# Windowed attention followed by an ELU feed-forward layer on one core: the first steps re-ordered around pair 3, one more subtraction on ScalarE, and the last products and rows cut another way

## The chip, the cores and the metric

The kernel runs on one core of a Trainium2 chip. The metric is the device time of one execution in microseconds. The core has TensorE (matrix products and the weight loads ahead of them), VectorE (called DVE in the profile), ScalarE (ACT), GpSimd (POOL) and SyncE (SP). Each engine takes its own instructions strictly in the order written; semaphores hold an instruction until what it reads is there. SP, ACT and POOL also issue DMA transfers, which all run on the core's 16 DMA engines.

## The reference

Attention for 8 batches and 8 heads of 576 positions by 64, where a position sees only those within 32 of it; then a feed-forward layer over the 4608 rows of 512, with an ELU between its two products.

```
scores = scale * q @ k.T ; masked where |i - j| > 32 ; attn = softmax(scores)
x   = (attn @ v), rows of all heads side by side     # 4608 x 512
h   = x @ w_in                                        # 512 -> 2048
g   = where(h > 0, h, exp(min(h, 0)) - 1)             # ELU
out = g @ w_out                                       # 2048 -> 512
```

The kernel computes the ELU as min(max(h, 0), exp(h) - 1), which is the same, and the products in bfloat16.

## The kernel before

**Attention in pairs.** The queries are cut into blocks of 64, 72 in all; two blocks make a pair (36 pairs), and a pair gives 128 rows of x. A pair goes through these functions: `scores` (16 narrow products, in two banks of PSUM), `exponential` on ACT, `mask` on DVE (a product with 0 and 1), `pv` (16 narrow products with the values, whose extra column of ones gives the sums), `normalize` on DVE (a reciprocal, then a product), `x_transpose` on TensorE (four transposes into PSUM) and `x_evac`, ACT's copy of them into the tile xT. Later pairs transpose by DMA. `rotate_v` makes on DVE the copy of the values shifted by 64 rows, V_o, in two parts, that the odd blocks read.

**The feed-forward layer in steps.** The rows go in 18 groups (t) of 256, two pairs each; 2048 hidden columns are cut into 8 steps of 256. That makes 144 steps. `order` says which group and slice step kk is: the first four slices of group 0, the first four of group 1, the other four of both in turn, then group by group. Step kk issues `mm1(kk)`: 8 products of 128 x 256 into the PSUM tile h0 or h1 (alternating), the exponential e_sb on ACT (L609), and the subtraction of 1, m_sb, on DVE (L615), for step 1 on ACT (L613). One step later `elu(kk)` forms g_sb on DVE (L626), which reads PSUM and frees it for `mm1(kk + 2)`. Two steps later `mm2(kk)` adds 4 products of 128 x 512 to the two PSUM tiles psY (L640). With the last slice of a group, `mm2` copies both blocks of 128 rows to SBUF, on ACT and DVE, and sends them out.

**Order around the change.** It is written out by hand. `at(kk, slot, fn, ...)` puts work into a step, and the main loop at the end runs for each kk: slot "first"; `elu(kk - 1)`; slot "dve"; `mm1(kk)`; slot "mid"; the products `mm2` that are due; slot "end". `mm2` runs two steps behind, with a table of exceptions for the first steps, since w_out's first quarter arrives late: none at 2 and 4, steps 0 and 1 at 3, steps 2 and 3 at 5. Pairs 0 and 1 are done before the loop; pairs 2 and 3 share steps 0 to 3 and make the rows of group 1, which step 4 reads first. `idle` is a number of products on zeros that only keep TensorE at work. They fill places where it waits.

The lines of pairs 2 and 3 before the change are L485 to L499. As written, DVE does at step 0 rotate part 0, mask of pair 2, rotate part 1, mask of pair 3, and only then, at step 1, the ELU of step 0; TensorE does mm1(0), the scores, mm1(1), four idle products, pv(2), two idle, pv(3), one idle, mm1(2), mm1(3), both pairs' transposes, then mm2(0) and mm2(1).

**Weights.** They come in quarters on POOL's queue, cast on the way: w_in's second quarter serves slices 2 and 3, which steps 2, 3, 6 and 7 read; w_out's first quarter serves slices 0 and 1, the `mm2` of steps 0, 1, 4 and 5. POOL issues them among loads of values; it waits for earlier transfers before it can issue more.

**The end.** The last step (143) has its PSUM in two tiles, of 128 hidden columns for 256 rows each, with two exponentials, subtractions and ELUs of half width. In the main loop the products of steps 142 and 143 are issued together: for the first row block (`ts` 0) those of both steps, then for the second. After each block its rows are copied out: the first by DVE, the second in two column halves, the left by DVE and the right by ACT, sent by SP and ACT.

Of the kernel before, what the change touches and what calls it, by code (L numbers as in the profile page):

```python
# [9 lines left out]
FP32 = mybir.dt.float32  # L10
# [11 lines left out]
def kernel(  # L22
# [9 lines left out]
    nc = tc.nc  # L32
# [5 lines left out]
    D_MODEL = H * D  # L38
# [8 lines left out]
    VS = 5  # L47
# [184 lines left out]
    def copy_on(eng, d_, s_):  # L232
        if eng is nc.scalar:
            nc.scalar.copy(d_, s_)  # L234
        else:
            eng.tensor_copy(d_, s_)  # L236
# [232 lines left out]
    def at(kk, slot, fn, *args):  # L469
        tasks.setdefault((kk, slot), []).append((fn, args))  # L470
# [15 lines left out]
    at(0, "mid", scores, 3, "u")  # L486
    for i in (2, 3):
        at(0, "mid", exponential, i)
    for i in (2, 3):
        at(0, "mid", rotate_v, 0, 2, VS - 1, (i - 2,))  # L490
        at(0, "mid", mask, i)

        at(1, "mid", idle, (4, 2)[i - 2], "y1")
        at(1, "mid", pv, i)
        at(2, "dve", normalize, i)
        at(3, "mid", x_transpose, i)
        at(3, "mid", x_evac, i, nc.scalar)
    at(1, "end", idle, 1, "y1")
    at(4, "dve", swap_pools)  # L499

    for part, kq in ((HALF_A, 7), (HALF_B, 15)):
# [86 lines left out]
    def mm1(kk):  # L588
        t, s = order[kk]
        h = kk % 2  # L590


        tags = (f"h{h}", "s") if kk == NSTEP - 1 else (f"h{h}",)
        w = FG // len(tags)
        psH[kk], m_t[kk] = [], []
        for z, tag in enumerate(tags):
            ps = ps_tile([128, w, TT], FP32, tag, "ps")
            psH[kk].append(ps)
            for j in range(w):
                fo = s * FG + z * w + j  # L600
                for do in range(NDO):
                    nc.tensor.matmul(  # L602
                        ps[:, j, :],
                        lhsT=w_in_sb[:, do, fo * 128:(fo + 1) * 128],
                        rhs=xT[t][:, :, do, :],
                        start=(do == 0), stop=(do == NDO - 1))
        for z, ps in enumerate(psH[kk]):
            e_sb = mpool.tile([128, w, TT], FP32, tag="e_sb", name="e_sb")
            nc.scalar.activation(e_sb, ps, AX.Exp)  # L609
            m_sb = mpool.tile([128, w, TT], BF16, tag="m_sb", name="m_sb")  # L610
            if kk == 1:

                nc.scalar.activation(m_sb, e_sb, AX.Copy, bias=-1.0)  # L613
            else:
                nc.vector.tensor_scalar(m_sb, e_sb, -1.0, None, ALU.add)  # L615
            m_t[kk].append(m_sb)
            if kk == NSTEP - 1:
                elu(kk, z)
# [10 lines left out]

    out_t = out.rearrange("(t ts p) c -> t p ts c", p=128, ts=TT // 128)  # L630

    def mm2(kk, parts=(0, 1)):
        t, s = order[kk]
        if s == 0:
            psY[t] = [ps_tile([128, D_MODEL], FP32, g, "psY")
                      for g in (("h2", "t0") if t == 1 else ("y0", "y1"))]
        last = t == NT - 1 and s == STEPS - 1
        for ts in parts:
            for j in range(FG):
                nc.tensor.matmul(  # L640
                    psY[t][ts],
                    lhsT=g_t[kk][:, j, ts * 128:(ts + 1) * 128],
                    rhs=w_out_sb[:, s * FG + j, :],
                    start=(s == 0 and j == 0),
                    stop=(s == STEPS - 1 and j == FG - 1))
        if last and s == STEPS - 1:


            for ts in parts:
                for z in range(1 + ts):  # L650
                    c = slice(z * D_MODEL // 2 * ts,
                              D_MODEL if z == ts else D_MODEL // 2)
                    eng = (nc.vector, nc.scalar)[z]
                    y_sb = opool.tile([128, D_MODEL], FP32,
                                      tag=f"y_sb{1 - z}", name="y_sb")
                    copy_on(eng, y_sb[:, c], psY[t][ts][:, c])
                    (nc.scalar if z else nc.sync).dma_start(
                        out_t[t, :, ts, c], y_sb[:, c])
        elif s == STEPS - 1:
            for ts in range(2):  # L660
                eng = (nc.scalar, nc.vector)[ts]
                y_sb = opool.tile([128, D_MODEL], FP32, tag=f"y_sb{ts}",
                                  name="y_sb")
                copy_on(eng, y_sb, psY[t][ts])
                nc.sync.dma_start(out_t[t, :, ts, :], y_sb)

    LAG = 2
    for kk in range(NSTEP + LAG):
        run(kk, "first")
        if 1 <= kk < NSTEP:  # L670
            elu(kk - 1)
        run(kk, "dve")
        if kk < NSTEP:
            mm1(kk)
        run(kk, "mid")

        for n in {2: (), 3: (0, 1), 4: (), 5: (2, 3)}.get(
                kk, (kk - LAG,) if kk >= LAG else ()):

            if n < NSTEP - 2:  # L680
                mm2(n)
            elif n == NSTEP - 1:
                for ts in range(2):
                    for m in (n - 1, n):
                        mm2(m, (ts,))
        run(kk, "end")


# [28 lines left out]
```

The softmax here doesn't subtract the row's maximum and nothing guards it: scores larger than these inputs give would overflow.

## Time and profile before

| what | value |
| --- | --- |
| median of 4 runs | 305.62 us (305.29 to 306.34) |
| profiled execution, its own time | 305.63 us |
| its span | 303.9 us |
| TensorE products, busy | 295.6 us, 97% |
| TensorE weight loads, busy | 197.2 us, 65% |
| VectorE busy | 242.4 us, 80% |
| ScalarE busy | 168.7 us, 56% |
| GpSimd busy | 48.2 us, 16% |
| granted TensorE clock | 1.00 |
| moved by DMA | 52.81 MB |

Times in the profile are microseconds from the start of the span. A row of the timeline gives the start, the length, the engine, the line of the kernel, the operation, the tile written and the tile read; "x8" means that eight like instructions are merged, and brackets give how long the engine stood idle before and what ended that. TensorE's products overlap, so a row's length holds the drain of the last one; how fast they follow each other is read from the starts. PEld is the weight load ahead of a product. The chain is followed back from the last instruction, at each step to what released it.

### The profile page before, as it was taken

How to read it: one execution, taken by the hardware profiler on the slowest of the kernel's cores; microseconds unless marked ns; L12 is line 12 of the kernel's file. 1: busy time of each engine (PE TensorE's matmuls, PEld its weight loads, DVE VectorE, ACT ScalarE, POOL GpSimd, SP SyncE). 2: the span in 40 equal slices, each digit the busy share in tenths (PEclk: the TensorE clock that was granted, in tenths of full speed). 3: DMA queues.
4: the chain of work that ended last, by engine and by line, in shares of the span. 5: the costliest groups of instructions: out<-in, count | busy, mean ns of one | idle time of the engine just before them, and what ended most of it. 6: DMA issues, size and time to landing. Idle time of an engine off the chain costs nothing.

```text
span 303.9 us, 7644 instructions
## 1 busy us (share of the span) xinstructions
PE 295.6 (97%) x3091; PEld 197.2 (65%) x3091; DVE 242.4 (80%) x473; ACT 168.7 (56%) x254; POOL 48.2 (16%) x68
## 2 busy tenths in 40 slices
PE   7799999999999999999999999999999999999995
PEld 2466666677666666666666666666666676666662
DVE  6876687978788887988798879887988787877664
ACT  3654656778664567546754675367545353534331
POOL 8836101820004100230023001300000000000000
PEclk9999999999999999999999999999999999999999
DMA  9999999999765997999799969996931111121011
GB/s 187 184 203 205 191 240 368 344 150 220 178 194 149 296 121 216 242 307 148 154 266 278 216 169 263 324 155 121 274 59 71 35 71 35 72 37 69 2 69 70
DMA packets 92117, 52.81 MB, mean 174 GB/s; under 512 B 76594, under 2 KB 81970, under 8 KB 92082
## 3 DMA queue, kind: packets, MB, share of 16 engines
q1 hardware_dynamic: 47330, 35.61, 43.6%
q0 software_dynamic: 42880, 10.10, 42.4%
q10 hardware_dynamic: 1872, 6.62, 5.8%
q8 instruction: 24, 0.39, 0.6%
q14 instruction: 11, 0.09, 0.1%
HBM read 36.70 MB, written 15.34 MB: 171 GB/s over the span
## 4 chain that ended last, share of the span: by engine, by line
PE 88%; DMA 4%; POOL 3%; DVE 2%; ACT 1%; issue 0%; DVEq 0%; POOLq 0%
PE psY L640 40%; PE ps L602 40%; DMA w_out_sb<-in_moe_w_out_dram 4%; PE psS L336 3%; PE psS L304 3%; POOL Ve L142 1%; PE ptx L279 1%; DVE g_sb L626 1%; POOL c L136 1%; PE psXT L357 1%; POOL w_in_sb L175 0%; DVE m_sb L615 0%; PE ptx L274 0%; ACT e_sb L609 0%; ACT pu L315 0%
## 5 line engine op out<-in xcount | busy, mean ns | idle before, releaser
L609 ACT ACTIVATE e_sb<-ps 128x512 f32<-128x512 f32 (+1 forms) x145 | 86.3, 595 | 119.6 <-PE ps L602 112.0
L602 PE MATMUL ps<-xT,w_in_sb 128*128 128x256 bf16 x1152 | 149.2, 273 | 0.1
L640 PE MATMUL psY<-w_out_sb,g_sb 128*128 128x512 bf16 x576 | 147.5, 379 | 0.2 <-DVE g_sb L626 0.2
L602 PEld LDWEIGHTS <-w_in_sb 128*128 128x128 bf16 x1152 | 110.7, 98 | 38.4 <-DMA w_in_sb<-in_moe_w_in_dram 0.8
L626 DVE SCALAR_TENSOR_TENSOR g_sb<-ps,m_sb 128x512 bf16<-128x512 f32 (+1 forms) x145 | 99.4, 686 | 12.6
L615 DVE TENSOR_SCALAR m_sb<-e_sb 128x512 bf16<-128x512 f32 x144 | 61.9, 430 | 37.9 <-ACT e_sb L609 36.1
L640 PEld LDWEIGHTS <-g_sb 128*128 128x128 bf16 x576 | 54.6, 98 | 39.2 <-DVE g_sb L626 0.6
L142 POOL DMA_DIRECT2D Ve<-in_v_dram x40 | 35.4, 896 | 138.6 <-PE psS L336 79.9
L315 ACT ACTIVATE pu<-psS 128x1024 bf16<-128x1024 f32 x36 | 36.5, 1020 | 1.6 <-PE psS L304 1.6
L348 DVE TENSOR_TENSOR x_st<-psS,rc 128x512 bf16<-128x512 f32 x36 | 24.9, 691 | 1.2
L324 DVE TENSOR_TENSOR pm<-pu,masks 128x1024 bf16<-128x1024 bf16 x36 | 24.6, 683 | 0.6 <-ACT pu L315 0.5
L234 ACT CAST qkb<-f 128x768 bf16<-128x768 f32 (+1 forms) x29 | 25.0, 860 | 0.0
L336 PEld LDWEIGHTS <-pm 128*64 128x64 bf16 x576 | 11.2, 110 | 10.0 <-DVE pm L324 8.8
L336 PE MATMUL psS<-Ve,pm 128*64 128x65 bf16 x320 | 13.6, 196 | 0.9 <-ACT pu L315 0.8
L236 DVE COPY y_sb<-psY 128x512 f32<-128x512 f32 (+1 forms) x19 | 12.7, 670 | 1.0 <-PE psY L640 1.0
L304 PEld LDWEIGHTS <-kT 64*128 64x128 bf16 x576 | 9.6, 95 | 4.9 <-issue 4.0
L336 PE MATMUL psS<-Vo,pm 128*64 128x65 bf16 x256 | 12.0, 196 | 0.2 <-DVE Vo L153 0.2
L304 PE MATMUL psS<-qT,kT 64*128 64x64 bf16 x576 | 11.8, 191 | 0.5 <-DVE kT L236 0.5
L234 ACT COPY y_sb<-psY 128x512 f32<-128x512 f32 (+1 forms) x18 | 10.3, 571 | 3.0 <-DVE y_sb L236 3.0
L153 DVE COPY Vo<-Ve 64x1040 bf16<-64x1040 bf16 x24 | 11.2, 467 | 0.8
L395 PE MATMUL ps_idle<-zeros 128*128 128x512 bf16 x27 | 9.0, 460 | 1.3 <-DVE zeros L194 1.3
L234 ACT COPY qT<-ptx 128x1152 bf16<-128x1152 bf16 (+2 forms) x8 | 7.5, 969 | 3.7 <-PE ptx L279 2.9
(36 smaller groups left out, 71.4 us busy)
## 6 DMA issues: line engine op xcount, KB each, us to landing
out_dram<-y_sb SPq DMA_DIRECT2D x35, 256.0 KB, 3.3
f<-in_q_dram SPq DMA_DIRECT2D x12, 576.0 KB, 5.8
f<-in_k_dram SPq DMA_DIRECT2D x12, 576.0 KB, 8.1
in_dram<-qkb ACTq DMA_DIRECT2D x10, 576.0 KB, 4.2
Ve<-in_v_dram POOLq DMA_DIRECT2D x24, 128.0 KB, 11.3
w_in_sb<-in_moe_w_in_dram POOLq DMA_DIRECT2D x4, 512.0 KB, 10.6
w_out_sb<-in_moe_w_out_dram POOLq DMA_DIRECT2D x4, 512.0 KB, 12.7
Ve<-in_v_dram POOLq DMA_DIRECT2D x16, 96.0 KB, 10.6
```

The source lines that it names most:

```text
L142: nc.gpsimd.dma_start(out=V_e[b % 3][p0:p1, m, :, 0:D], in_=v[b, :, lo + p0:lo + p1, :].rearrange("h p d -> p h d"))
L234: nc.scalar.copy(d_, s_)
L304: nc.tensor.matmul(psS[:, h % 2, hp * 128 + z * QB:hp * 128 + (z + 1) * QB], lhsT=kT[b % 2][base:base + 64, KPAD + hp * S + QB * qb - WIN: ...
L315: nc.scalar.activation(pu, _bap(psS, [psS.ap[0], [1, 1024]]), AX.Exp, scale=SCALE)
L324: nc.vector.tensor_mul(pm, pu, _bap(mm, [mm.ap[0], [0, H], [1, 2 * QB]]))
L336: nc.tensor.matmul(psS[QB * z:QB * (z + 1), par, hp * VD:(hp + 1) * VD], lhsT=pm[:, par * HP + hp, z * QB:(z + 1) * QB], rhs=vv[:, qb // 2 ...
L348: nc.vector.tensor_mul(x_st, _bap(psS, [psS.ap[0], [VD, HP], [512, 2], [1, D]]), _bap(rc, [rc.ap[0], [2, HP], [1, 2], [0, D]]))
L602: nc.tensor.matmul(ps[:, j, :], lhsT=w_in_sb[:, do, fo * 128:(fo + 1) * 128], rhs=xT[t][:, :, do, :], start=(do == 0), stop=(do == NDO - 1))
L609: nc.scalar.activation(e_sb, ps, AX.Exp)
L615: nc.vector.tensor_scalar(m_sb, e_sb, -1.0, None, ALU.add)
L626: nc.vector.scalar_tensor_tensor(g_t[kk][:, z * w:(z + 1) * w, :], ps, 0.0, m_t[kk][z], ALU.max, ALU.min)
L640: nc.tensor.matmul(psY[t][ts], lhsT=g_t[kk][:, j, ts * 128:(ts + 1) * 128], rhs=w_out_sb[:, s * FG + j, :], start=(s == 0 and j == 0), sto ...
```

## The change

For pairs 2 and 3: on DVE the ELU of step 0 comes ahead of pair 3's mask. On TensorE, pv(3) goes behind mm1(2), the idle product after it is gone, and pair 3's transposes go behind mm2(0). Pair 3's normalization follows pv(3) in step 2. The subtraction of step 2 moves to ACT, so that two steps have it there. At the end, mm2 of step 142 is issued whole and then that of step 143. The first row block's copy stays whole on DVE; of the second, ACT now takes the left half and DVE the right.

```diff
--- before.py
+++ after.py
@@ -486,16 +486,21 @@
     at(0, "mid", scores, 3, "u")
     for i in (2, 3):
         at(0, "mid", exponential, i)
+    at(0, "mid", rotate_v, 0, 2, VS - 1, (0,))
+    at(0, "mid", mask, 2)
+    at(0, "mid", rotate_v, 0, 2, VS - 1, (1,))
+    at(1, "dve", mask, 3)
+
+    at(1, "mid", idle, 4, "y1")
+    at(1, "mid", pv, 2)
+    at(1, "mid", idle, 2, "y1")
+    at(2, "dve", normalize, 2)
+    at(2, "mid", pv, 3)
+    at(2, "mid", normalize, 3)
     for i in (2, 3):
-        at(0, "mid", rotate_v, 0, 2, VS - 1, (i - 2,))
-        at(0, "mid", mask, i)
-
-        at(1, "mid", idle, (4, 2)[i - 2], "y1")
-        at(1, "mid", pv, i)
-        at(2, "dve", normalize, i)
         at(3, "mid", x_transpose, i)
         at(3, "mid", x_evac, i, nc.scalar)
-    at(1, "end", idle, 1, "y1")
+        at(3, "mid", lambda n: mm2(n), i - 2)
     at(4, "dve", swap_pools)
 
     for part, kq in ((HALF_A, 7), (HALF_B, 15)):
@@ -608,7 +613,7 @@
             e_sb = mpool.tile([128, w, TT], FP32, tag="e_sb", name="e_sb")
             nc.scalar.activation(e_sb, ps, AX.Exp)
             m_sb = mpool.tile([128, w, TT], BF16, tag="m_sb", name="m_sb")
-            if kk == 1:
+            if kk in (1, 2):
 
                 nc.scalar.activation(m_sb, e_sb, AX.Copy, bias=-1.0)
             else:
@@ -629,13 +634,13 @@
 
     out_t = out.rearrange("(t ts p) c -> t p ts c", p=128, ts=TT // 128)
 
-    def mm2(kk, parts=(0, 1)):
+    def mm2(kk):
         t, s = order[kk]
         if s == 0:
             psY[t] = [ps_tile([128, D_MODEL], FP32, g, "psY")
                       for g in (("h2", "t0") if t == 1 else ("y0", "y1"))]
         last = t == NT - 1 and s == STEPS - 1
-        for ts in parts:
+        for ts in range(2):
             for j in range(FG):
                 nc.tensor.matmul(
                     psY[t][ts],
@@ -646,16 +651,15 @@
         if last and s == STEPS - 1:
 
 
-            for ts in parts:
-                for z in range(1 + ts):
-                    c = slice(z * D_MODEL // 2 * ts,
-                              D_MODEL if z == ts else D_MODEL // 2)
-                    eng = (nc.vector, nc.scalar)[z]
-                    y_sb = opool.tile([128, D_MODEL], FP32,
-                                      tag=f"y_sb{1 - z}", name="y_sb")
-                    copy_on(eng, y_sb[:, c], psY[t][ts][:, c])
-                    (nc.scalar if z else nc.sync).dma_start(
-                        out_t[t, :, ts, c], y_sb[:, c])
+            half = D_MODEL // 2
+            for ts, c0, n, z in ((0, 0, D_MODEL, 1), (1, 0, half, 0),
+                                 (1, half, half, 1)):
+                y_sb = opool.tile([128, D_MODEL], FP32, tag=f"y_sb{z}",
+                                  name="y_sb")
+                copy_on((nc.scalar, nc.vector)[z], y_sb[:, c0:c0 + n],
+                        psY[t][ts][:, c0:c0 + n])
+                (nc.scalar, nc.sync)[z].dma_start(
+                    out_t[t, :, ts, c0:c0 + n], y_sb[:, c0:c0 + n])
         elif s == STEPS - 1:
             for ts in range(2):
                 eng = (nc.scalar, nc.vector)[ts]
@@ -674,15 +678,9 @@
             mm1(kk)
         run(kk, "mid")
 
-        for n in {2: (), 3: (0, 1), 4: (), 5: (2, 3)}.get(
+        for n in {2: (), 3: (), 4: (), 5: (2, 3)}.get(
                 kk, (kk - LAG,) if kk >= LAG else ()):
-
-            if n < NSTEP - 2:
-                mm2(n)
-            elif n == NSTEP - 1:
-                for ts in range(2):
-                    for m in (n - 1, n):
-                        mm2(m, (ts,))
+            mm2(n)
         run(kk, "end")
```

In the changed kernel the main loop calls `mm2(n)` for every step, two steps behind, as it did before for the steps up to 141.

## Prediction

> **What bounds the kernel now.** I read the page first: the busy shares, then the chain that ended last.
>
> ```profile
> PE 295.6 (97%) x3091; PEld 197.2 (65%) x3091; DVE 242.4 (80%) x473; ACT 168.7 (56%) x254; POOL 48.2 (16%) x68
> PE 88%; DMA 4%; POOL 3%; DVE 2%; ACT 1%; issue 0%; DVEq 0%; POOLq 0%
> ```
>
> TensorE is busy throughout and makes 88% of the chain; the one other large link is a transfer. So only what TensorE waits for counts. The chain in order of time, for the first 30 us, tells where that transfer ends (start, length, what):
>
> ```profile
> 11.23 12.04 DMA w_out_sb<-in_moe_w_out_dram
> 23.27 0.04 issue
> 23.31 1.89 PE psY L640 x8
> 25.20 1.75 PE ps L602 x16
> ```
>
> The first quarter of w_out lands just before 23.31, and from there the chain stays on TensorE until its last steps: time lost or won at 23.31 goes through to the end, and time won ahead of 23.31 is worth nothing. The timeline around it (start, length, engine, line, what; idle time before it in brackets):
>
> ```profile
> 19.20 0.69 DVE L324 TENSOR_TENSOR pm<-pu,masks 128x1024 bf16<-128x1024 bf16 x1
> 19.80 1.28 DVE L626 SCALAR_TENSOR_TENSOR g_sb<-ps,m_sb 128x512 bf16<-128x512 f32 x2
> 20.10 0.34 PEld L336 LDWEIGHTS <-pm 128*64 128x64 bf16 x16 [0.42 <-DVE pm L324]
> 20.49 0.39 PE L395 MATMUL ps_idle<-zeros 128*128 128x512 bf16 x1
> 20.79 1.64 PEld L602 LDWEIGHTS <-w_in_sb 128*128 128x128 bf16 x16 [0.21 <-DMA w_in_sb<-in_moe_w_in_dram]
> 22.55 0.67 PE L357 MATMUL psXT<-ident,x_st 128*128 128x128 bf16 x8
> 23.24 1.07 ACT L234 COPY xT<-psXT 128x512 bf16<-128x512 bf16 x2
> 23.31 1.89 PE L640 MATMUL psY<-w_out_sb,g_sb 128*128 128x512 bf16 x8
> 25.03 1.91 PE L602 MATMUL ps<-xT,w_in_sb 128*128 128x256 bf16 x16
> ```
>
> Pair 3's values (20.10) and an idle product (20.49) stand in time in which step 2 couldn't start: its weights, w_in's second quarter, end the wait at 20.79. The eight transposes of pairs 2 and 3 start at 22.55; eight products from 23.31 to 25.03 take 0.215 each, a transpose of four takes 0.22 (41.46 to 41.68 at pair 4), so the eight stream until 22.99. TensorE then waits 0.32 us for w_out: that is cover.
>
> The tail, from the timeline, and the last 3 us by stretches (length; busy time of PE, PEld, DVE, ACT, POOL; clock, DMA share, GB/s):
>
> ```profile
> 299.06 1.25 PE L640 MATMUL psY<-w_out_sb,g_sb 128*128 128x512 bf16 x5 [0.16 <-DVE g_sb L626]
> 299.49 0.69 DVE L236 COPY y_sb<-psY 128x512 f32<-128x512 f32 x1 [0.48 <-PE psY L640]
> 300.35 0.42 DVE L236 COPY y_sb<-psY 128x256 f32<-128x256 f32 x1 [0.17 <-PE psY L640]
> 300.81 0.37 ACT L234 COPY y_sb<-psY 128x256 f32<-128x256 f32 x1 [2.99 <-DVE y_sb L236]
> 301.21 0.35 ACTq L657 DMA_DIRECT2D out_dram<-y_sb  x1
> ```
>
> ```profile
> 301.00:301.50 0.50, 0.00 (x0) 0.00 (x0) 0.00 (x0) 0.18 (x1) 0.00 (x0) 1.00 0.94 352
> 301.50:302.00 0.50, 0.00 (x0) 0.00 (x0) 0.00 (x0) 0.00 (x0) 0.00 (x0) 1.00 0.95 340
> 302.00:302.50 0.50, 0.00 (x0) 0.00 (x0) 0.00 (x0) 0.00 (x0) 0.00 (x0) 1.00 0.97 338
> ```
>
> The 512 KB of the last two row blocks stream without a gap from about 301.07 (0.87 after the first issue at 300.20) to 302.53, at 0.94 to 0.97 of the transfer engines. Their end is set by when the first block starts, and hardly by when the last piece is issued.
>
> **The change, part by part.** The profiled execution took 305.63 us, 1.73 around its span of 303.9; the median of the four runs is 305.62, so both give the same base.
>
> *Pair 3's values behind step 2.* VectorE now does the ELU of step 0 at 19.20 (0.69) and pair 3's mask after it, until about 20.6; TensorE no longer waits for that mask ahead of step 2. Step 2 still needs its weights. POOL's wait for the same transfer ends at 21.03; at two other landings POOL came 0.48 and 0.52 us after TensorE (15.74 against 15.26, 23.83 against 23.31), so I bound the start of step 2 by 20.55 and 20.79. What follows now is step 2 (0.87), pair 3's values, step 3 (0.87), pair 2's transposes (0.22). The values cost 0.34 for sixteen weight loads and 0.10 for the switch to narrow tiles: at pair 4's scores the products before them end at 36.91 and they start at 37.01. That is 2.40 us, ending between 22.95 and 23.19: still ahead of w_out, 0.12 us at least. So the added 0.44 costs nothing, covered by the 0.32 of waiting and the 0.22 of transposes that went behind. If step 2 started after 20.91, the excess would show one for one.
>
> *Pair 3's transposes between the two products.* Steps 0 and 1's products were 1.72 us on end. Now four transposes stand between them: +0.22, with no cover, since w_out has landed by then. Step 4 would start at 25.25 in place of 25.03. It also needs pair 3's rows out of PSUM: the transposes end at 24.17 + 0.39, ACT's copy takes 0.58 (the one at 14.57) and ends at 25.18, so it fits by 0.07. I take +0.22; bounds 0.1 (landing a little earlier) and 0.6 (the copy late by 0.4).
>
> *Subtraction of step 2 on ACT.* DVE's row is 0.43 (L615), ACT's only row of this kind, step 1's, 0.63 (L613). Queued behind it on ACT are step 3's exponential and both copies to xT. Step 2's products end by 21.83 at the latest, so exponential 22.47, subtraction 23.10; step 3's products end at 23.14 by the same count, so its exponential is not held. On DVE, pair 2's normalization (0.9) follows the ELU of step 1 from 21.3, pair 3's ends by 23.2, the ELU of step 2 by 23.95. Step 4 overwrites that PSUM tile only at 25.25. Cost 0, cover 1.3 us; step 3's own ELU then ends about 25.1 and its reader is the second product group at 27.
>
> *The idle products.* One fewer (0.21 of TensorE), in time that now is a wait before step 2: 0. Without it the wait lasts up to 0.8 us. The granted clock is 1.00 in every row of before; yet the first ten idle products took 4.12 us, 0.41 each, against 0.215 later, so a slow TensorE costs a factor of two. The nearest row to a gap is that between the pairs' values and weights here, some 0.5 us without loss. I take 0, bounded above by half speed for some 3 us, +1.5.
> The Trainium skill, "TensorE: Matmul & The Clock Gate" (section "Why this matters for your kernels"), says that idle gaps up to about 3 us keep the clock; by it this bound falls away and the sum stays.
>
> *Queues.* POOL's order of transfers is the same, so w_out lands where it did. SP's order differs only in which half it sends last, ACT's queue gets one issue, earlier.
>
> *Last products by steps.* Before: seven products from 297.23, then a wait for the last ELU half until 299.06, then five. Now that wait is filled: the first row block gets its last product as the tenth of twelve, 297.23 + 9 x 0.215 = 299.17, against 299.06, so its copy and its transfer come 0.11 later; the second block's last product starts at 299.60 instead of 299.94, 0.34 earlier.
>
> *The two halves.* ACT copies its half first (300.03 to 300.40), then DVE (after the first copy, 300.29, and ACT's) until 300.86; last issue about 300.88 against 301.21. By the issue alone that is -0.33. But the transfer engines are full: the first block starts at 301.18, the halves are there before it is through, and 512 KB take 1.46 as before. So +0.10; bounds -0.33 and +0.2, and I take +0.10, because the share of 0.94 to 0.97 leaves no gaps that an earlier issue could fill.
> A page of the Trainium skill, "DMA: Bandwidth & Descriptors" (section "Specifications"), gives a ceiling of 435 GB/s; at that rate 512 KB would take an estimated 1.2 us, the old last half would have waited for its issue, and the tail would come out at 0.0, the sum at +0.22. The rows show 338 to 352 GB/s.
>
> **Sum.** +0.22 (head) + 0.10 (tail) = +0.32: 305.63 + 0.32 = 305.95 us. All between stays, shifted: TensorE's rows there follow each other, and the later weights land early (POOL's wait for w_in's third quarter ends at 31.50, step 8 reads it at 32.71).
>
> **Rivals.**
> *The tail goes by its last issue* (-0.33): for it, ACT's copy sat 2.99 us and the last issue moves 0.33; against it, the full transfer engines. 305.63 + 0.22 - 0.33 = 305.5.
> *Both ends gain.* If w_out is not what holds 23.31, but the order of TensorE ahead of it, the first products start as early as 22.95, -0.36 there, +0.22 for the transposes, -0.33 at the tail: 305.15. Against: TensorE had its weights loaded at 23.00 and did nothing. A gain above 0.9 would need w_out itself 0.5 us earlier besides, 304.7; I see no cause, only scatter.
> *A slower head: the copy of pair 3's rows.* ACT's queue carries step 2's subtraction ahead of it, and DVE's carries three more operations ahead of pair 3's normalization. If pair 3's x rows came after 24.17 rather than 23.2, step 4 would wait for each 0.1 of it; with 0.7 lost there, 305.63 + 0.32 + 0.7 = 306.65. The point that decides: ACT's second copy to xT ending later than step 1's product stream.
> *A slower clock* after the wait ahead of step 2: +1.5 less the 0.3 of cover, 305.63 + 0.32 + 1.2 = 307.15.
> *The change does nothing* by itself: that is within the first case's range.
>
> **How the numbers follow.** Forecast 0.48 (305.95, own range 305.5 to 306.4), tail gain 0.17, both gain 0.11, late copy 0.13, slower clock 0.11. A measurement tells about 0.3% (0.92 us) from no change: below 304.7 or above 306.54. Faster takes most of "both gain" with luck, 0.10; slower the last two and a little of the first, 0.29; the same 0.61. The range from 305.2 to 307.0 leaves out the lower half of "both gain" and the upper part of the clock case.
>
> **What would show it.** Right: first products again near 23.3, four transposes between them, step 4's first product about 0.2 later; last product about 0.3 earlier against the step before it, first output issue about 0.1 later, no gap in the transfers to the end. Wrong: products of step 0 well off 23.3 either way; TensorE waiting for xT at step 4; products of 0.41 after 20 us; a shorter time from the first output issue to the end.

## Result and the profile after

The changed kernel takes 306.16 us (median of 31 runs, 305.57 to 307.95), the kernel before 305.5 us (51 runs, 304.95 to 306.95). The ratio is 1.0022, 95% interval [1.0015, 1.0029]: some 0.66 us slower, clear of zero and inside the 0.3% that the prediction called no change. It had 305.95.

The sum came out near; its two terms did not. The head of the kernel (its first steps), forecast at +0.22, came out at -0.34 in the run that has it alone (interval -0.67 to -0.03). The tail (its end), forecast at +0.10, costs 0.95 in the profile and 0.52 in the run that has it alone (interval 0.12 to 0.92).

The page after, first its busy row and then the chain's shares by engine:

```profile
PE 295.1 (97%) x3090; PEld 197.2 (65%) x3090; DVE 241.6 (80%) x472; ACT 169.6 (56%) x255; POOL 48.9 (16%) x68
...
PE 91%; DMA 2%; POOL 2%; DVE 2%; ACT 1%; issue 0%; POOLq 0%; DVEq 0%
```

One idle product fewer on PE, and one subtraction that has gone from DVE (473 to 472 instructions) to ACT (254 to 255). TensorE's share of the chain went from 88% to 91%, and that of transfers from 4% to 2%: the step from w_out's landing to the first products is no longer in it. That holds for this one execution: in six of the eight other profiles of the new order the first products start within 0.07 of w_out's landing (see the head, below). The chain of the changed kernel in order of time (start, length, what):

```profile
18.39 0.44 DVE Vo L153
18.82 0.04 issue
18.87 0.42 PE psS L336 x15
19.29 0.54 PE ps_idle L395 x2
19.82 0.87 PE ps L607 x8
20.70 0.38 PE psS L336 x16
21.08 0.98 PE ps L607 x8
22.06 0.22 PE psXT L357 x4
22.28 0.86 PE psY L645 x4
23.14 0.22 PE psXT L357 x4
23.37 0.86 PE psY L645 x4
24.23 1.75 PE ps L607 x16
```

From 18.87 on TensorE runs without a gap: pair 2's values, two idle products, step 2, pair 3's values (0.38), step 3, four transposes, four products, four transposes, four products, step 4. No transfer and no copy holds it. (The chain places a product some 0.15 later than the timeline does; below, starts are the timeline's, where step 4 begins at 24.07 against 25.03 before.)

The end, from the timeline (start, length, engine, line, what; idle time before in brackets):

```profile
296.29 2.75 PE L645 MATMUL psY<-w_out_sb,g_sb 128*128 128x512 bf16 x12
...
298.64 1.26 DVE L236 COPY y_sb<-psY 128x512 f32<-128x512 f32 x2 [0.58 <-PE psY L645]
299.07 0.37 ACT L234 COPY y_sb<-psY 128x256 f32<-128x256 f32 x1 [2.21 <-PE psY L645]
299.36 0.90 SPq L661 DMA_DIRECT2D out_dram<-y_sb  x2
299.48 0.36 ACTq L661 DMA_DIRECT2D out_dram<-y_sb  x1
```

Counted from step 143's first product (295.41 here, 296.36 before), the twelve products are through after 3.63, before after 3.95; the first output is issued after 3.95, before after 3.84. Both are what the prediction named: the last product 0.32 earlier, the first send 0.11 later. Then the transfers. By stretches (length; busy time of PE, PEld, DVE, ACT, POOL; clock, DMA share, GB/s), and the issues of the last 5 us (KB, us from issue to landing):

```profile
300.50:301.00 0.50, 0.00 (x0) 0.00 (x0) 0.00 (x0) 0.00 (x0) 0.00 (x0) 1.00 1.00 365
301.00:301.50 0.50, 0.00 (x0) 0.00 (x0) 0.00 (x0) 0.00 (x0) 0.00 (x0) 1.00 0.99 336
301.50:302.00 0.50, 0.00 (x0) 0.00 (x0) 0.00 (x0) 0.00 (x0) 0.00 (x0) 1.00 0.41 141
302.00:302.50 0.50, 0.00 (x0) 0.00 (x0) 0.00 (x0) 0.00 (x0) 0.00 (x0) 0.84 0.01 2
302.50:303.00 0.50, 0.00 (x0) 0.00 (x0) 0.00 (x0) 0.00 (x0) 0.00 (x0) 0.50 0.00 0
```

```profile
q14 instruction: 1, 0.01, 0.4%
...
out_dram<-y_sb SPq DMA_DIRECT2D x1, 256.0 KB, 2.1
out_dram<-y_sb ACTq DMA_DIRECT2D x1, 128.0 KB, 2.3
out_dram<-y_sb SPq DMA_DIRECT2D x1, 128.0 KB, 3.0
```

The transfer engines are full until about 301.7 and empty from there on, yet the last half needs 3.0 us to land and SP waits for it until 302.98. SP's waits for the outputs at the end, before and then after (us in all, times, longest):

```profile
SPq L712 <- DMA out_dram<-y_sb: 1.4, 3, 0.7
```

```profile
SPq L710 <- DMA out_dram<-y_sb: 2.2, 3, 1.1
```

What happens from 301.7 on is in the trace's packets. A transfer goes over the 16 transfer engines; at the end of its share each of them adds one to the transfer's counter with a packet of 4 bytes (48 of them for the three last transfers), and SP waits for all sixteen. After the changed kernel's data are all but through, one packet of another queue starts:

```
after, packets of the transfer engines, last ones
301.77 to 301.82   queue 1 (SP)            1024 bytes
301.78 to 301.79   queue 1 (SP)               4 bytes   (counter)
301.81 to 302.12   queue 14 (instruction)  8192 bytes
302.12 to 302.17   queue 1 (SP)            1024 bytes
302.16 to 302.17   queue 1 (SP)               4 bytes   (counter)
counter of the last half: 15th share seen at 302.13, 16th and last at 302.96

before
302.57 to 302.62   queue 10 (ACT)          1024 bytes
302.62 to 302.62   queue 10 (ACT)             4 bytes   (counter)
303.05 to 303.35   queue 14 (instruction)  8192 bytes
counter of the last half: 15th share seen at 302.94, 16th and last at 302.96
```

Both kernels fetch 8 KB of instructions once in their last microseconds. Before, the fetch came 0.43 after the data's end. After, it came while one transfer engine still had its last piece of the last half to write, and that engine's share, the straggler below, was seen 0.83 later than the fifteenth. (The trace doesn't name a packet's engine; that the late piece stood behind the fetch is read from its start, which lies within 0.01 of the fetch's end here and in e2, e6, e9 and e11.) The kernel can't end before it.

The two executions with a profile took 305.63 (before) and 305.60 (after): alone they would say "same". Of the difference of their parts, step 0 starts 0.34 earlier after (14.92 against 15.26, by the arrival of its weights, which no edit touches), step 0 to step 4 is 0.62 shorter, step 4 to step 143 is 0.02 longer, step 143 to the end 0.95 longer (8.48 against 7.53): -0.34 - 0.62 + 0.02 + 0.95 = 0.01, while the medians are 0.66 apart. The profiled execution of after is one of its fastest runs, and the one of before has, as the runs below show, a head that is slower than most.

### The profile page after: what moved, and what is told of

It reads as the page before. It is cut to its first block, busy times and chain, and to the rows that moved or that the text cites. A ratio compares the mean times of both kernels' runs of the same rounds, so it can differ in the third digit from the quotient of the medians.

```text
span 303.9 us, 7640 instructions
## 1 busy us (share of the span) xinstructions
PE 295.1 (97%) x3090; PEld 197.2 (65%) x3090; DVE 241.6 (80%) x472; ACT 169.6 (56%) x255; POOL 48.9 (16%) x68
## 4 chain that ended last, share of the span: by engine, by line
PE 91%; DMA 2%; POOL 2%; DVE 2%; ACT 1%; issue 0%; POOLq 0%; DVEq 0%
PE ps L607 41%; PE psY L645 41%; PE psS L336 4%; PE psS L304 3%; DMA w_in_sb<-in_moe_w_in_dram 2%; PE ptx L279 1%; POOL Ve L142 1%; POOL c L136 1%; PE psXT L357 1%; DVE Vo L153 0%; DVE pm L324 0%; PE ptx L274 0%; ACT e_sb L614 0%; ACT pu L315 0%; DVE m_sb L620 0%
## 5 line engine op out<-in xcount | busy, mean ns | idle before, releaser
L620 DVE TENSOR_SCALAR m_sb<-e_sb 128x512 bf16<-128x512 f32 (+1 forms) x143 | 62.2, 435 | 36.9 <-ACT e_sb L614 35.0
L153 DVE COPY Vo<-Ve 64x1040 bf16<-64x1040 bf16 x24 | 10.4, 432 | 1.1 <-DMA Ve<-in_v_dram 0.3
```

## Experiments

Each kernel computes the whole output, and each left a profile. This table has one row for each: the stretches from the first product of step 0 to that of step 2, of step 2 to 4, of step 0 to 4; how long after the landing of its weights (w_in's second quarter) step 2 starts; from step 143's first product to the end; when the fetch of instructions starts, counted from the first output issue; how many packets of the outputs start after the fetch; and when the last share of any output is seen, counted from the fetch. All in us. Step 4 to step 143 is 271.32 to 271.39 in all.

| kernel | head | tail | 0 to 2 | 2 to 4 | 0 to 4 | step 2 after weights | 143 to end | fetch | packets after it | last share after it |
|---|---|---|---|---|---|---|---|---|---|---|
| before | old | old | 5.53 | 4.24 | 9.77 | 0.05 | 7.53 | 2.85 | 0 | -0.09 |
| after | new | new | 4.74 | 4.41 | 9.15 | 0.25 | 8.48 | 2.45 | 2 | 1.15 |
| e1 | new | old | 4.76 | 4.46 | 9.22 | 0.05 | 7.54 | 2.73 | 0 | 0.03 |
| e2 | old | new | 6.01 | 4.07 | 10.08 | 0.68 | 8.46 | 2.44 | 2 | 1.15 |
| e3 | old | products by steps | 5.33 | 4.07 | 9.40 | 0.41 | 7.73 | 2.54 | 0 | 0.25 |
| e4 | old | new halves | 5.35 | 4.07 | 9.42 | 0.83 | 7.73 | 2.43 | 0 | 0.52 |
| e5 | new | new, queues exchanged | 5.30 | 4.47 | 9.76 | 0.05 | 7.75 | 2.49 | 0 | 0.33 |
| e6 | new | new, 8 small loads | 4.92 | 4.41 | 9.33 | 0.27 | 8.52 | 2.49 | 1 | 1.15 |
| e7 | new, subtraction on DVE | old | 4.90 | 4.48 | 9.38 | 0.05 | 7.54 | 2.75 | 0 | 0.02 |
| e8 | old, no idle product | old | 5.16 | 4.25 | 9.40 | 0.22 | 7.55 | 2.72 | 0 | 0.05 |
| e9 | new | new, 1 small load | 4.89 | 4.41 | 9.30 | 0.14 | 8.95 | 2.49 | 1 | 1.15 |
| e10 | new | old, first copy on ACT | 4.62 | 4.41 | 9.03 | 0.30 | 8.24 | 2.05 | 141 | 1.52 |
| e11 | new | new, DVE busy longer | 4.69 | 4.47 | 9.15 | 0.05 | 8.48 | 2.46 | 2 | 1.14 |
| e12 | new | new, ACT busy longer | 4.62 | 4.41 | 9.03 | 0.12 | 8.19 | 2.09 | 97 | 1.23 |

### The change in its parts: e1 to e4

Four kernels take the change apart: the head alone, the tail alone, and each of the tail's two edits alone. The theory was the prediction's: head +0.22, tail +0.10.

e1 (before, with the change's new order of the first four steps and step 2's subtraction on ACT; the end is the old one):

```
+    at(1, "dve", mask, 3)
+    at(2, "mid", pv, 3)
     ...
+        at(3, "mid", lambda n: mm2(n), i - 2)
-    at(1, "end", idle, 1, "y1")
-            if kk == 1:
+            if kk in (1, 2):
```

> The first four steps as in the change (ELU of step 0 ahead of pair 3's mask, pair 3's values behind step 2, its transposes between the products of steps 0 and 1, step 2's subtraction on ACT), the end as before. By the forecast's terms +0.22 us (ratio 1.0007), whatever w_out's landing. By a second theory, that the end carries the whole loss, the head is 0 or a gain: where w_out lands early (21.9 us, as in the changed kernel's profile) the old order would itself be late, and the new one gains 0.3; so -0.3 to +0.2 (1.0000 within 0.0008).

Measured: 305.26 us, ratio 0.9989 [0.9978, 0.9999]: about 0.34 us faster than before, where 0.22 slower (1.0007) was forecast. The interval excludes the forecast, and only just excludes no change. Its tail is that of before, 7.54.

e2 (before, with both of the tail's edits):

```
-        for ts in parts:
+        for ts in range(2):
     ...
+            for ts, c0, n, z in ((0, 0, D_MODEL, 1), (1, 0, half, 0),
+                                 (1, half, half, 1)):
     ...
-                for ts in range(2):
-                    for m in (n - 1, n):
-                        mm2(m, (ts,))
+            mm2(n)
```

> The first steps as before; last products by steps and the new halves. By the forecast +0.10 us (ratio 1.0003), last issue to last landing 2.1 us as before. By the second theory +0.5 to +0.9 (1.0016 to 1.0030), and in the profile the last of the three transfers lands 0.8 us after the others' pace, on one DMA engine that an instruction fetch of 8 KB holds; by the rival of the prediction (the last issue decides) -0.33 (0.9989).

Measured: 306.36 us, ratio 1.0017 [1.0004, 1.0030]. Slower by 0.52 (0.12 to 0.92), more than the 0.10 forecast, and with the same late share as after (1.15 after the fetch).

e3 (only the products by steps, the old halves) and e4 (only the new halves, the old order of products):

```
e3
-            if n < NSTEP - 2:
-                mm2(n)
-            elif n == NSTEP - 1:
-                for ts in range(2):
-                    for m in (n - 1, n):
-                        mm2(m, (ts,))
+            mm2(n)
e4
+            for ts, c0, n, z in ((0, 0, D_MODEL, 1), (1, 0, half, 0),
+                                 (1, half, half, 1)):
+                if ts not in parts:
+                    continue
```

> Only the last products by steps; each half of the last rows is copied and sent by the engine that did it before (left by DVE and SP, right by ACT). By the forecast: first output issue 0.11 us later, transfers without a gap, +0.10 us (1.0003). If the loss comes from the new halves, 1.0000 to 1.0003; if it comes from the later start of the first block, all of +0.6 is here (1.0020).

> Only the new halves: of the second row block ACT copies and sends the left half first, DVE and SP the right one after; products as before. By the forecast 0 (1.0000), since the transfers have no gap. If the order of the two halves' sends makes the last landing late, +0.5 to +0.8 (1.0016 to 1.0026) here and nothing in the run with the steps alone.

Measured: e3 305.51, ratio 1.0003 [0.9988, 1.0018]; e4 305.48, ratio 0.9995 [0.9986, 1.0003]. Neither edit costs what both cost together. e3 sends its last piece 0.16 earlier against step 143 than before (4.69 against 4.85 us after its first product) and gains nothing by it. In their profiles the fetch falls 0.10 after the data (e3) or level with their end (e4, less than 0.01 before it, with no packet left to start), and the tail is 7.73, 0.20 above before. The two 0.20 differ: in e3 no share is late, in e4 the last share comes 0.19 after the fifteenth. e4's interval leaves room for little of that.

What follows: the loss is in the tail, and it needs both edits. The parts don't add up well: by their ratios e1 and e2 together give +0.18, while the whole measures +0.66; the intervals of the parts just allow it. And after, with the new head, is no faster than e2, with the old head and the same tail (1.0022 against 1.0017). So the head's gain is shown by e1 alone, and its size is open.

### The head: e7, e8, and step 2 in all profiles

e7 is e1 with step 2's subtraction left on DVE; e8 is before without the one idle product ahead of step 2:

```
e7, against e1
-            if kk in (1, 2):
+            if kk == 1:
e8, against before
-    at(1, "end", idle, 1, "y1")
```

> The head alone, but the subtraction of step 2 stays on DVE. The forecast costs that move at 0 with 1.3 us of cover: so the same as the head alone (0.9989), within 0.0008. If the move to ACT is what pays for the head's gain, 1.0000 or above.

> The kernel before without the one idle product ahead of step 2. The forecast: step 2 is held by its weights, so 0.0 us (1.0000). The theory from the new profiles (step 2 started at 20.55 and 20.62 us with w_in's second quarter landed at 19.72 and 20.21): step 2 is held by pair 3's mask, values and the idle product in most executions, so up to -0.21 us (0.9993); a slower clock would show as +0.5 or more.

Measured: e7 305.36, ratio 0.9987 [0.9967, 1.0007], as e1's: the subtraction's place is worth nothing that shows, and from step 2 to 4 the two profiles take 4.48 and 4.46. e8 305.57, ratio 1.0003 [0.9978, 1.0027]: no gain shows, though the interval is too wide to exclude the 0.21 of an idle product. In e8's profile step 2 does start earlier than in before (5.16 after step 0 against 5.53), but TensorE then waits for another:

```profile
20.27 1.91 PE L601 MATMUL ps<-xT,w_in_sb 128*128 128x256 bf16 x16
22.02 0.39 PE L357 MATMUL psXT<-ident,x_st 128*128 128x128 bf16 x4
22.56 0.40 PE L357 MATMUL psXT<-ident,x_st 128*128 128x128 bf16 x4 [0.15 <-DVE x_st L348]
22.79 1.89 PE L639 MATMUL psY<-w_out_sb,g_sb 128*128 128x512 bf16 x8
```

Pair 3's transposes wait for its rows from DVE, and the products follow them (w_out's first quarter had landed at 22.57): from step 2 to 4 it takes 4.25 where e3 and e4 take 4.07, so 0.18 of the 0.21 of an idle product is given back.

The column "step 2 after weights" says what ends the wait before step 2. With the new order step 2 follows its weights by 0.05 to 0.30. With the whole old order it did so in the profile of before (0.05) and in no other: 0.41, 0.68, 0.83 in e3, e2 and e4. There step 2 stands behind pair 3's values and the idle product, as the timeline of e3 shows (weights landed at 20.21):

```profile
20.01 0.22 PE L336 MATMUL psS<-Ve,pm 128*64 128x65 bf16 x1
...
20.39 0.39 PE L395 MATMUL ps_idle<-zeros 128*128 128x512 bf16 x1
20.62 1.91 PE L602 MATMUL ps<-xT,w_in_sb 128*128 128x256 bf16 x16
22.36 0.76 PE L357 MATMUL psXT<-ident,x_st 128*128 128x128 bf16 x8
22.96 1.89 PE L640 MATMUL psY<-w_out_sb,g_sb 128*128 128x512 bf16 x7
24.69 1.91 PE L602 MATMUL ps<-xT,w_in_sb 128*128 128x256 bf16 x16
```

And the case of the prediction, weights that land late, with the new order, is in e5's profile (5.25 after step 0, in before 5.48):

```profile
21.02 1.05 PE L607 MATMUL ps<-xT,w_in_sb 128*128 128x256 bf16 x8 [0.51 <-DMA w_in_sb<-in_moe_w_in_dram]
...
22.38 1.05 PE L607 MATMUL ps<-xT,w_in_sb 128*128 128x256 bf16 x8
23.26 0.39 PE L357 MATMUL psXT<-ident,x_st 128*128 128x128 bf16 x4
23.53 1.02 PE L645 MATMUL psY<-w_out_sb,g_sb 128*128 128x512 bf16 x4
24.39 0.39 PE L357 MATMUL psXT<-ident,x_st 128*128 128x128 bf16 x4
24.62 1.03 PE L645 MATMUL psY<-w_out_sb,g_sb 128*128 128x512 bf16 x4
```

Step 2 waits 0.51 for its weights, and from step 2 to step 4 takes 4.47, 0.23 more than in before: the forecast's +0.22, to 0.01.

A second landing decides what this is worth: that of w_out's first quarter, which the first products need. In all fourteen profiles it comes 2.52 to 2.54 after w_in's second quarter, and both transfers are issued before 12.0, while the first instruction that the edit moves runs at about 19. So the landings scatter from profile to profile (w_in's second quarter 4.33 to 5.48 after step 0) whatever the order, and the order is compared by what follows them:

| from w_out's landing | to the first product that reads it | to step 4 |
|---|---|---|
| old order: before | 0.04 | 1.77 |
| old order: e2, e3, e4 | 0.51, 0.23, 0.64 | 2.23, 1.96, 2.37 |
| new order: e1, e5, e7, e9, e11, e12 | 0.04 to 0.07 | 1.99 to 2.02 |
| new order: after, e6, e10 | 0.18 to 0.23 | 2.13 to 2.18 |

With the new order w_out's landing is what starts the first products in six of nine profiles, with early and with late weights, and from it to step 4 they take some 0.23 more than before did: the forecast's head. But the old order starts its first products so close to w_out only in the profile of before; in e2, e3 and e4 step 2 comes late by the order itself, and the first products 0.23 to 0.64 after w_out is there. What the change is worth goes with the landing of w_in's second quarter. Where it comes 4.33 to 4.51 after step 0, the time from step 0 to 4 is 9.03 to 9.15 with the new order (after, e10, e12) and 9.42 with the old (e4). At 4.85 and 4.92 it is 9.38 (e7) and 9.40 (e3). At 5.25 it is 9.76 with the new order (e5), at 5.33 and 5.48 with the old 10.08 (e2) and 9.77 (before). So early weights favour the new order by 0.27 to 0.39 (against a single old profile), and late ones don't decide.

How much that is on average the profiles don't fix: from w_out's landing to step 4 their means are 2.05 for the nine of the new order and 2.08 for the four of the old, far less than e1's 0.34, though two of the four drew late weights, where the old order has the least to lose.

### The straggler: e5 and e6

e5 exchanges the queues of the two halves, so that the last half is the only transfer on ACT's queue and not the second on SP's. e6 puts eight unneeded one-element loads on SP's queue at step 132, which lengthen SP's program and so might move the fetch.

```
e5, against after
-                (nc.scalar, nc.sync)[z].dma_start(
+                (nc.scalar if c0 else nc.sync).dma_start(
e6, against after
+    for _ in range(8):
+        at(132, "end", gate, w_in_at(3))
```

> The changed kernel, with the sends of the last two halves exchanged between the queues: ACT's half goes out on SP's queue, DVE's half, the last, on ACT's. Theory of the fetch: in the changed kernel an instruction fetch of 8 KB starts 0.36 us after SP passes the first block's landing and goes ahead of the last half, which is on SP's queue, on one DMA engine; that engine's share lands 0.82 us after the other fifteen. Where the last half is on ACT's queue (before, and the run with the head alone) the fetch came behind the data. So here the last landing is complete within 0.2 us of its fifteen first shares and the time is 0.5 to 0.8 us below the changed kernel's 306.16 (ratio to before 0.998 to 1.0000). If the loss came from the later start of the first block alone, it stays at 1.0017 to 1.0025.

> The changed kernel, with eight more one-element transfers on SP's queue some 25 us before the end, so that SP's instructions stand elsewhere against the blocks in which they are fetched. Theory of the fetch: the fetch of 8 KB moves from the middle of the last transfers to an earlier place, the last landing is complete within 0.2 us, and the time is 0.5 to 0.8 us below the changed kernel's (ratio to before 0.998 to 1.0000). If the fetch isn't what holds the last share, the straggler stays at 0.8 us and the ratio at 1.0017 to 1.0025.

Measured: e5 305.64, ratio 0.9995 [0.9976, 1.0013]: with the whole change but this one line the loss is gone, as far as the interval tells, which lies just below that of after. (The medians of its rounds, 305.64 against 305.41 for before, differ by +0.23; e6, in the same rounds, differs by +1.14.) Its tail in the profile is 7.75 (that execution, 306.31, is the slowest of its twelve by the late weights at its head), and the last landing has no late share (fifteenth 303.56, sixteenth 303.61). Its issues, to be held against those of after:

```profile
out_dram<-y_sb SPq DMA_DIRECT2D x1, 256.0 KB, 2.1
out_dram<-y_sb SPq DMA_DIRECT2D x1, 128.0 KB, 2.0
out_dram<-y_sb ACTq DMA_DIRECT2D x1, 128.0 KB, 2.2
```

The fetch comes 0.06 after the last data there: the margin is thin, and that most executions without a profile keep to the good side of it is read from the ratio alone.

e6 306.55, ratio 1.0026 [1.0007, 1.0045]: a miss. The fetch came at 2.49 after the first issue, no earlier, so the eight loads didn't bring it forward (2.45 in after); the straggler stayed (1.15).

### What sets the fetch off: e9 to e12

Four more runs ask what triggers it. e9 adds one unneeded small load, which turns round the order in which SP waits for the outputs, so that SP stands at the first wait until the last half is in; if SP's passing of its waits sets off the fetch, it must come later. e10 is e1 with the first block copied by ACT, so that the first output starts early with the old queues. e11 and e12 are after with three unneeded operations behind the last copy of DVE, or behind ACT's last send, which keep that engine busy until 301.19 (DVE, in after 299.90) and 302.11 (ACT, in after 299.44).

```
e9, against after
+    at(132, "end", gate, w_in_at(3))
e10, against e1
-                    eng = (nc.vector, nc.scalar)[z]
+                    eng = nc.scalar if ts == 0 else (nc.vector, nc.scalar)[z]
e11 and e12, against after, at the end
+    late = mpool.tile([128, 512], FP32, tag="e_sb", name="late")
+    for _ in range(3):
e11     nc.vector.tensor_scalar(late, zeros, 1.0, None, ALU.add)
e12     nc.scalar.activation(late, zeros, AX.Exp)
```

> The changed kernel with one more one-element transfer on SP's queue 25 us before the end. The completion counters go round in turn, so the last half now has the counter that SP waits for first at the end of the program, the first block the one before the last. Theory of the fetch (it is started by SP getting past its next to last waits, and goes ahead of the last half's share on one DMA engine): SP can't get there before the last half has landed, so the last landing is complete within 0.15 us of its fifteenth share, the fetch comes after it, the stretch from step 143 to the end is 7.7 to 7.8 us in place of 8.48, and the ratio to before 0.999 to 1.0005. If the straggler has another cause (the last half being on SP's queue by itself), it stays: 8.4 to 8.5 us, ratio 1.0015 to 1.0025.

> The change's first steps, the old products and halves at the end, and the first row block copied by ACT (0.58) instead of DVE (0.69): its transfer starts 0.11 us earlier. If the end goes by the start of the first block, since the transfers have no gap, the stretch from step 143 to the end is 7.43 in place of 7.54 us, and the ratio 0.9985 (0.9989 for the head alone less 0.0004). If the last issue decides, 7.54 and 0.9989.

> The changed kernel with three unneeded operations on DVE behind its last copy (some 1 us, off the path of the output), so that DVE comes to the end of its program about 1 us later. If the late fetch of 8 KB belongs to DVE's coming to its end, it moves by about 1 us, behind the data, the last landing has no straggler, and the stretch from step 143 to the end falls from 8.48 to 7.7 us (ratio to before 0.9995). If it belongs to another engine, the fetch stays about 1.62 us after the first output data and the stretch at 8.4 to 8.5 us (1.0022).

> The same on ACT: three unneeded activations behind ACT's last send (some 1.8 us), off the path of the output. If the fetch belongs to ACT's coming to its end, it moves behind the data and the stretch falls to 7.7 us (0.9995); if not, it stays at 8.4 to 8.5 us (1.0022).

Measured: e9 306.89 (5 runs), ratio 1.0046 [1.0032, 1.0060]. The waits of SP at its end:

```profile
SPq L712 <- DMA out_dram<-y_sb: 2.7, 1, 2.7
```

One wait of 2.7 us, until 303.88, and the fetch still starts at 302.71: SP's passing of its waits doesn't set it off. SP's seven other waits then follow the long one, 0.06 apart, instead of standing beside the transfers; the program ends 1.36 after the last landing instead of 0.93, which makes the tail 8.95.

e10 305.87, ratio 1.0015 [1.0005, 1.0026], tail 8.24: both expectations, 7.43 and 7.54, missed. The fetch came at 301.44, in the midst of the data (141 packets after it), and two landings have a late share (301.84 to 302.65 on SP's queue, 302.23 to 302.96 on ACT's). So the queue of the last half doesn't protect it; the time of the fetch against the data decides.

e11 305.98, ratio 1.0018 [1.0009, 1.0028]: nothing moved; DVE's end doesn't set it off. e12 305.81, ratio 1.0008 [0.9999, 1.0017]: the fetch came earlier, not later (2.09 after the first issue against 2.45), and the last share came 0.55 after the fifteenth instead of 0.83, tail 8.19. So it isn't ACT's end either. That the work on ACT moved it is read from one profile.

What the four leave standing is the pattern in the table's last two columns. In every profile in which no packet of the outputs starts after the fetch, the tail is 7.53 to 7.75. In every one in which at least one does, it is 8.19 to 8.95. Where one or two packets are left, the last share is seen 1.14 to 1.15 after the fetch's start, in five kernels out of five. The border isn't sharp: in e4 the last counter packet starts less than 0.01 before the fetch, and its share is still 0.19 late.

What triggers the fetch stays open: it starts 0.94 to 1.92 after the last output issue and 2.05 to 2.85 after the first, and neither is fixed. A kernel without that fetch was not tried.

## Why the prediction was right or wrong

**The whole.** 305.95 against 306.16, inside the range of 305.2 to 307.0, and no change by the bound of 0.3%. That the amount is near is in part luck: two errors of opposite sign cancel. The head was 0.56 too high (+0.22 against -0.34 by e1's ratio), the tail 0.85 too low by its profile (+0.10 against +0.95) and 0.42 too low by e2's ratio (0.52). With the profile's tail the parts give -0.34 + 0.95 = 0.61, with e2's +0.18, against 0.66 measured; the noise of the parts doesn't let more be said.

**"Step 2 still needs its weights", with the old order waiting for them too: the step of the head that failed.** It was read from one execution, in which w_in's second quarter landed at 20.74 (so the lower bound of 20.55 for step 2 wasn't possible there). In most others it lands up to a microsecond earlier, and the old order itself, pair 3's mask, values and idle product, held step 2 by 0.41 to 0.83 and the first products by 0.23 to 0.64 past w_out's landing. The rival "Both ends gain" named this: not w_out but the order of TensorE ahead of it holds the first products. Set against it was that TensorE waited with its weights loaded, which was true of this execution only. Its other half, a gain at the tail, didn't come.

**Values ahead of w_out, covered by 0.32 of waiting and 0.22 of transposes: right for the new order in most profiles.** In six of nine the first products start within 0.07 of w_out's landing, so the values cost nothing there; in the other three they start 0.18 to 0.23 after it. The wait itself was 0.26 rather than 0.32: the last of the eight transposes starts at 23.00 and they are some 0.055 apart, so they stream until 23.05, not 22.99.

**Transposes between the products, +0.22; pair 3's rows in time: right.** The chain has the four transposes with 0.22 between two groups of 0.86. ACT's copy of pair 3's rows runs from 23.40 to 23.98, and step 4 starts at 24.07: the fit was forecast at 0.07 (by the prediction's own terms, 24.17 + 0.39 + 0.58 = 25.14, it would have been 0.11) and is 0.09. The rival of the late copy didn't come.

**Subtraction on ACT and idle product, 0 each: nothing speaks against it.** For the subtraction e7 and e1 agree; e8's interval is too wide to settle the idle product. Its cover was not the one named: in e8's profile, where the weights are early, pair 3's rows take up what step 2 wins. From 14 to 26 us the granted clock is 1.00 in every profile; the slower clock didn't come.

**Tail: the steps of TensorE and of the first send were right to 0.01 or 0.02** (last product 0.32 earlier against 0.34 forecast, first output 0.11 later against 0.11), and so was "hardly by when the last piece is issued": after and e2 send their last piece 0.33 earlier against step 143, e3 0.16, and none is faster by it, which rules out the rival "the tail goes by its last issue". What failed is the sentence "the halves are there before it is through, and 512 KB take 1.46 as before", +0.10 with bounds of -0.33 and +0.2. The data did take their time, but the landing is not the end of the data. The term left out an instruction fetch that runs on the same transfer engines and that was there before as well, 0.43 behind the data. Counted from step 143's first product, the data end at 6.26 before and, but for the one late piece, at 6.41 after; the fetch starts at 6.69 before and at 6.40 after. So the two met because the data ended 0.15 later and the fetch came 0.29 earlier; what moved the fetch is not known. I had read the share of the transfer engines (0.94 to 0.97) and not what else ran on them, nor how long after the last packet the landing was seen. Of the +0.95, 0.20 to 0.22 stays without the straggler, which is the upper bound: in e3 and e5 the first output is issued 0.11 later, from there the last landing takes 0.03 to 0.06 longer, and from the landing the program's end 0.05 to 0.06 longer. About 0.73 is then the straggler.

The Trainium skill bears on how one packet costs 0.83: "DMA: Bandwidth & Descriptors", section "Why a DMA increments its semaphore by 16 and not by 1", says that a transfer is done only when each engine taking part has written its increment, and its section "Queues, rings and completion order" says that this increment lands only after every earlier write of that engine, from other queues too. The packets of after agree with both: elsewhere the counter's 4 bytes are seen 0.34 after their packet (before: 302.62 to 302.96), behind the fetch 0.79 (302.17 to 302.96), and the time from the fetch to the last share is the same 1.14 to 1.15 in five kernels. 0.38 is then waiting for the fetch's packet and some 0.45 waiting for the fetch's own write. That the increment waits for that write fits these numbers; no run here separates it from another cause, and e4, whose last counter packet starts ahead of the fetch and is late by 0.19 all the same, doesn't fit so neatly.

**What stays open:** what starts the fetch; whether every execution without a profile has the straggler (the ratios of after, e2, e6 and e11 suggest that most do); and how large the head's gain is: e1's 0.34 is more than the profiles show, and after against e2 shows none. Of the kernels run, e1, the new head with the old end, is the only one whose interval lies below 1: 0.9989 [0.9978, 0.9999], ahead of both kernels.

## What to carry to other kernels

A wait that ends on a transfer in one profile is one draw: the same landing moved by some 1.1 us between these profiles, so price a reordering for the early landing as well as for the late one, and ask what would hold the step if the transfer came first. At the end of a kernel, count to the moment when the last share of the last transfer is seen, not to the end of the data: list every packet of the last microseconds, foreign queues too, and keep the data's end clear of them. An edit that brings work forward by a few tenths can cost more than it gains when the end of a transfer comes to meet something that was out of its way.

## What the runs showed of the hardware

- An instruction fetch of 8 KB shares the transfer engines with the data. It took 0.31 to 0.49 us, and where one 1 KB piece and its counter packet came behind it (after), the landing was 0.83 late.
- The time of that fetch is not fixed to the end of any engine that was tried: SP held for 2.7 us left it in place, longer work on DVE too, and with longer work on ACT it came 0.36 earlier against the first output's issue (one profile each).
- In fourteen profiles w_out's first quarter landed 2.52 to 2.54 after w_in's second quarter, while the two together scattered by 1.1 us against step 0.
- With the transfer engines full, 512 KB of output ran at 336 to 365 GB/s. In after the granted clock fell to 0.84 and 0.50 between 302.0 and 303.0, some 3 us after TensorE's last product (299.04), with nothing left for it to slow down.
